# Two layer boundaries and the order of one VectorE step in a talking-heads attention with two MLPs

## The chip, the core and the metric

The kernel runs on one core of one Trainium2 chip. TensorE multiplies into PSUM, ScalarE and VectorE move and transform, GpSimd does a little elementwise work, and SyncE's queue issues nearly all DMAs. Each engine takes its instructions strictly in program order. The metric is device microseconds of one execution, median of 3 runs. A profiled execution adds a trace; its span leaves out the small time around the program.

## What is computed

```python
scores = scale * np.matmul(q, k.transpose(0, 1, 3, 2))     # 4 batches, 12 heads, 448 rows, 64 wide
scores = np.einsum('bhij,hg->bgij', scores, w_pre)         # heads mixed before the softmax
scores = scores - np.max(scores, axis=-1, keepdims=True)
attn = np.exp(scores)
attn = attn / (np.sum(attn, axis=-1, keepdims=True) + 1e-09)
attn = np.einsum('bhij,hg->bgij', attn, w_post)            # heads mixed after it
x = np.matmul(attn, v)                                     # -> 1792 rows of 768
h = x @ w_in;  g = np.where(h > 0, h, np.exp(np.minimum(h, 0)) - 1);  x = g @ w_out
h = x @ w_in2; r = np.maximum(h, 0); out = (r * r) @ w_out2       # both 768 -> 2048 -> 768
```

The MLP weights arrive as 64-bit floats, 768 x 2048 and 2048 x 768 for each of the two MLPs.

## The kernel before

**Attention** runs in T = 90 steps s of two row groups each. A step multiplies the pre-mix of step s+2 on TensorE (`mix_pre`, line 182, into two `ps_mix` banks; there are only two), then part of A·V of an earlier chunk (`values`, line 254), the post-mix of step s (`mix_post`, line 218, into two `ps_post` banks) and the scores of a later chunk (line 156). On VectorE a step holds, in program order: `weigh(s+1)`, which adds 1e-9 to the sums (`tot`, line 197) and takes their reciprocal (`rec`, line 199), after which GpSimd multiplies the mixing weights (`wg`, line 202); `maxima(s+2)`, two row maxima from `ps_mix` (`nmax`, line 190), after which ScalarE takes two exponentials (`ex`, line 192), which free the `ps_mix` banks for the next `mix_pre`; and the copies of the post-mix out of PSUM (`at`, line 236). At the end of a chunk ScalarE and VectorE also add up two A·V banks (`xs`, lines 262 and 263).

**The weights** are a list of units (`Weights`). A unit goes through `load` (DMA of the 64-bit words, `wd`), `size` (ScalarE, line 453), `turn` (four VectorE operations, lines 477 to 483, that make a 32-bit float `wf` of the 64-bit one), `part_hi` and `part_lo` (a high part `wh` cast by ScalarE, line 524, and the rest `wl` by VectorE, line 531). Each product is three matmuls: high x high, low x high, high x low (lines 670 to 672). `next()` calls `advance(i)` before unit i is used: it loads up to unit i+6, sizes up to i+5, turns up to i+4 and parts up to i+3, so the work of later units stands in the queues ahead of whatever the program does next. Turned units are also stored (`w1if<-wf`) for the second half of the rows.

**The first boundary.** In the last steps of the attention `plan` loads, sizes and turns units of the first MLP and multiplies the first two of them (`begin`, which takes both `ps_qk` banks). `inner(0)` then begins with output block f = 1 and unit 2; f = 0 is only activated (Relu and Exp on ScalarE, lines 690 and 692, then line 697 on VectorE, which frees the `ps_qk` bank that f = 2 takes next).

**The second boundary.** `outer_first` multiplies the hidden layer of the first half of the rows by w_out: six output blocks o, eight units each. After a block its two PSUM banks are split into the second MLP's input, `xh` (ScalarE, line 675) and `xl` (VectorE, line 676). `inner(1)` multiplies by the second MLP's units, k = 0 to 5 for each f, so its first f needs the split of o = 5 for k = 5. Beside both layers run 16 units of the last matrix (`load_beside`, `size_beside`): each is turned in step with another unit, which doubles the four operations of that `turn`.

Of the kernel before, what the change touches and what calls it, by code (L numbers as in the profile page):

```python
# [52 lines left out]
def attention(tc, dram, psum, qr, kr, vr, w_pre, w_post, diagonal, xd, mlps):  # L53
# [7 lines left out]
    with ExitStack() as ctx:  # L61
# [123 lines left out]
        def maxima(s):  # L185
            tot[s] = work.tile([128, 2], F32, name="tot", bufs=3)
            ex[s] = []
            for r, p in enumerate(mixed.pop(s)):
                nmax = work.tile([128, 1], F32, name="nmax", bufs=4)
                nc.vector.tensor_reduce(nmax, p, AX.X, ALU.max, negate=True)  # L190
                e = work.tile([128, S], F32, name="ex", bufs=2 * (MIX + 1))
                nc.scalar.activation(e, p, AF.Exp, bias=nmax, scale=1.0, accum_out=tot[s][:, r : r + 1])  # L192
                ex[s].append(e)

        def weigh(s):
            sums = tot.pop(s)
            nc.vector.tensor_scalar_add(sums, sums, 1e-9)
            rec = work.tile([128, 2], F32, name="rec", bufs=3)
            nc.vector.reciprocal(rec, sums)
            w = work.tile([128, 2, HALF], F32, name="wg", bufs=3)  # L200
            shape = [128, 2, HALF]
            nc.gpsimd.tensor_tensor(
                w, post.rearrange("p g r -> p (g r)").unsqueeze(1).broadcast_to(shape), rec.unsqueeze(2).broadcast_to(shape),
                ALU.mult,
            )
            wg[s] = w
# [60 lines left out]
        def store_x(s):  # L267
            while stored and stored[0][0] <= s:
                _, o, x = stored.pop(0)
                nc.sync.dma_start(out=o, in_=x)  # L270
# [74 lines left out]
        for s in range(T + 3):  # L345
            beside = extra.pop(s, ())
            pairs = [a for f, a in beside if f is scores]
            if s + 1 < T:
                weigh(s + 1)
            for x in gathers.get(s, ()):  # L350
                gather(x)
            if s + MIX < T:
                mix_pre(s + MIX)
                maxima(s + MIX)
            store_x(s)
            pieces = [a for f, a in beside if f is values]
            for a in pieces[:-1]:
                values(*a)
            if s < T:
                mix_post(s, 0)  # L360
            for a in pairs[:1]:
                scores(*a)
                keep_scores()
            if s < T:
                mix_post(s, 1)
                keep_weighed(s == T - 1)
            for a in pieces[-1:]:
                values(*a)
            for a in pairs[1:]:
                scores(*a, *((("pv", "pv"),) if s < values_from else ()))  # L370
                keep_scores()
            keep_x(s)
            for f, a in beside:
                if f not in (scores, values):
                    f(*a)
# [197 lines left out]
class Mlps:  # L573
# [25 lines left out]
    def plan(self, put, T, last, work, early_ctx, score_ctx):  # L599
        w = self.weights  # L600

        def start():
            early_ctx.close()
            score_ctx[2].close()
            score_ctx[1].close()
            self.xp = self.pool("xp", "right")
            self.tp = self.pool("tp", "right")
            self.nx = self.two_parts(KC, self.xp, "x", MOVING)
            self.xraw = {}

        def start_weights():
            score_ctx[0].close()
            w.pool = self.pool("wp", "right")
            w.pool.tile([128, 8], F32, name="room")
            self.raw_ctx = self.ctx.enter_context(ExitStack())
            w.raw_pool = self.pool("wr", "right", self.raw_ctx)

        for i in range(2):
            put(last - 8 + i, w.load, lambda: work.tile([128, 384, 2], I32, name="wd0", bufs=2))
            put(last - 5 + i, w.size, lambda: work.tile([128, 384], F32, name="wf0", bufs=2))  # L620
            for k in range(4):
                put(last - 4 + 2 * i + k // 2, w.turn_op, k)
        put(last, start)
        for i in range(2 * KC):
            put(last + i // 2, self.load_x, i)
            put(last + 3 + i // 2, self.split_x, i)
        put(last + 1, w.flush)
        put(T - 4, start_weights)
        for i in range(2):
            put(T - 4, w.part_hi)  # L630
            put(T - 4, w.part_lo)
            put(T - 3 + i, w.load)
            put(T - 1 + i, w.size)
            put(T - 1 + i, w.turn)
        for i in range(4):
            put(T - 3 + min(i, 2), self.begin, i)

# [213 lines left out]
    def outer_first(self, xh, xl, hh, hl):  # L851
        nc = self.nc
        for o in range(KC):
            p = [self.bank()[:, :S] for _ in self.BLOCKS]
            for f2 in range(FC // 2):
                wh, wl = self.weights.next()
                if f2 == 1:
                    self.weights.load_beside()
                if f2 == 4:
                    self.weights.size_beside()  # L860
                for j, bl in enumerate(self.BLOCKS):
                    for i in range(2):
                        f = 2 * f2 + i
                        self.three(p[j], wh[:, col(i)], wl[:, col(i)], hh[:, f, bl], hl[:, f, bl], f == 0, f == FC - 1)
            for j, bl in enumerate(self.BLOCKS):
                self.split(xh[:, o, bl], xl[:, o, bl], p[j])
# [233 lines left out]
    def run(self):  # L1100
        with ExitStack() as ctx:
            hp = self.pool("hp", "left", ctx)
            hh, hl = self.two_parts(FC, hp, "h", MOVING)
            self.inner(0, *self.nx, self.keep_parts(hh, hl))
            x = self.two_parts(KC, self.xp, "x", MOVING)
            self.outer_first(*x, hh, hl)
        self.hq = self.pool("hq", "left")
        w = self.weights

        def beside(f):  # L1110
            if f > 1 and w.aside:
                w.size_beside()
            if f % 3 != 2 and w.beside:
                w.load_beside(lambda: self.hq.tile([128, S + 32, 2], I32, name="wb", tag="rh", bufs=4))

        self.hr = {}
        self.start_split(STATIONARY)
        self.inner(1, *x, self.keep_raw, beside)
        x = self.outer_last(0)
        self.hr = {}  # L1120
        self.start_split(MOVING)
        self.seven(0, x)
        x, carry = self.outer_combos()
        self.hr = {}
        self.halves = {}
        self.seven(1, x, carry)
        self.seven_last()
# [49 lines left out]
```

## Time and profile before

| | us |
|---|---|
| median of 3 runs (lowest, highest) | 1265.84 (1263.19, 1271.76) |
| the profiled execution | 1264.1 |
| its span | 1262.3 |
| busy in the span: TensorE, VectorE, ScalarE, GpSimd | 1220.5, 990.5, 695.6, 52.5 |

A row of the timeline gives start, duration, engine and line, operation, output<-inputs, and in brackets how long the engine was idle before it and what it had waited for. Rows of one kind that follow each other are merged (x2). Matmuls overlap, so their durations are longer than the distance of their starts. TensorE's clock has two levels here, 2.4 GHz (granted clock 1.00) and 1.2 GHz (0.50); a stretch between shows both.

### The profile page before, as it was taken

The numbers are of one execution on the slowest core, as the hardware profiler recorded it, in microseconds if no ns is written. First come the engines' busy times: TensorE is split into PE (matmuls) and PEld (weight loads), VectorE is DVE, ScalarE is ACT, GpSimd is POOL, SyncE is SP. The second block draws the span as 40 slices with busy tenths as digits, with TensorE's granted clock in tenths as the row PEclk, the third lists the DMA queues.
The fourth block names the chain that finished last, engine by engine and source line by source line (L and its number), as shares of the span: only waits on it lengthen the run. The fifth ranks groups of instructions, "written<-read, shape, count | busy, mean of one in ns | idle before, by whom it ended". The sixth has DMA issues, their size and how long they took to land.

```text
span 1262.3 us, 35367 instructions
## 1 busy us (share of the span) xinstructions
PE 1220.5 (97%) x14223; PEld 1088.2 (86%) x14224; DVE 990.5 (78%) x2104; ACT 695.6 (55%) x1537; POOL 52.5 (4%) x118
## 2 busy tenths in 40 slices
PE   8899989999889999999899999999999999999998
PEld 4677667677679999998799999999999998999998
DVE  4576767677859998788899996868896758888876
ACT  4666666666637774333444454646673535455654
POOL 1010111011410000000000000000000000000000
PEclk9899999999999999999999999999999999999999
DMA  6665645655735545666666555222137441223443
GB/s 177 210 202 184 212 158 184 213 174 191 213 114 177 175 155 157 190 187 194 218 240 206 202 175 178 73 94 76 50 113 243 152 144 34 68 63 101 126 132 119
DMA packets 137948, 197.93 MB, mean 157 GB/s; under 512 B 26712, under 2 KB 117176, under 8 KB 137784
## 3 DMA queue, kind: packets, MB, share of 16 engines
q1 hardware_dynamic: 137544, 195.38, 48.4%
q8 instruction: 112, 1.84, 0.6%
q14 instruction: 52, 0.43, 0.1%
q10 hardware_dynamic: 240, 0.29, 0.1%
HBM read 114.44 MB, written 42.47 MB: 124 GB/s over the span
## 4 chain that ended last, share of the span: by engine, by line
PE 78%; DVE 11%; ACT 6%; issue 3%; DMA 1%; SPq 0%; ACTq 0%; DVEq 0%
PE ps_qk L670 5%; PE ps_qk L671 5%; PE ps_qk L672 5%; PE ps_pv L672 5%; PE ps_pv L671 5%; PE ps_post L670 5%; PE ps_mix L672 5%; PE ps_pv L670 5%; PE ps_mix L671 5%; PE ps_post L672 5%; PE ps_post L671 5%; PE ps_mix L670 5%; PE ps_mix L182 4%; PE ps_post L218 4%; PE ps_pv L254 4%; PE ps_qk L156 3%
## 5 line engine op out<-in xcount | busy, mean ns | idle before, releaser
L524 ACT CAST wh<-wf 128x384 fp32r<-128x384 f32 (+1 forms) x304 | 149.6, 494 | 196.9 <-DVE wf L483 129.0
L531 DVE TENSOR_TENSOR wl<-wf,wh 128x384 fp32r<-128x384 f32 (+1 forms) x304 | 162.4, 537 | 53.5 <-ACT wh L524 51.8
L218 PEld LDWEIGHTS ps_post<-wg,ex 60*64 60x64 f32 x5040 | 138.3, 135 | 51.8 <-issue 31.5
L192 ACT ACTIVATE ex<-ps_mix,nmax 128x448 f32<-128x448 f32 x180 | 112.6, 630 | 112.9 <-DVE nmax L190 112.7
L236 DVE COPY at<-ps_post 128x420 f32<-128x420 f32 x178 | 97.6, 591 | 56.8 <-PE ps_post L218 56.6
L218 PE MATMUL ps_post<-wg,ex 60*64 60x60 f32 x5040 | 134.2, 220 | 6.1 <-issue 3.8
L182 PE MATMUL ps_mix<-graw,pre 64*64 64x448 f32 (+1 forms) x720 | 111.6, 553 | 11.4 <-ACT ex L192 7.8
L190 DVE TENSOR_REDUCE nmax<-ps_mix 128x1 f32<-128x448 f32 x180 | 104.6, 617 | 19.8 <-PE ps_mix L182 19.4
L676 DVE TENSOR_TENSOR rl<-hr,rh 128x896 fp32r<-128x896 f32 (+2 forms) x104 | 94.8, 914 | 25.6 <-ACT rh L675 25.6
L675 ACT CAST rh<-hr 128x896 fp32r<-128x896 f32 (+2 forms) x104 | 82.9, 799 | 48.6 <-PE ps_post L672 24.7
L254 PE MATMUL ps_pv<-at,v 64*64 64x110 f32 (+3 forms) x2976 | 97.8, 248 | 4.2 <-issue 2.1
L254 PEld LDWEIGHTS ps_pv<-at,v 64*64 64x64 f32 x2976 | 86.6, 133 | 14.5 <-issue 5.8
L156 PE MATMUL ps_qk<-kt,qt 64*64 64x448 f32 (+1 forms) x680 | 92.4, 546 | 4.4 <-issue 3.2
L453 ACT ACTIVATE wf<-wd 128x384 f32<-128x384 f32 (+1 forms) x134 | 68.1, 513 | 42.3 <-DMA wd<-w1o 22.0
L161 ACT COPY sc<-ps_qk 120x448 f32<-120x448 f32 x167 | 80.7, 539 | 12.9 <-PE ps_qk L156 12.7
L483 DVE SCALAR_TENSOR_TENSOR wf<-wd,wf 128x384 int32<-128x384 int32 (+1 forms) x134 | 67.8, 510 | 3.9
L481 DVE SCALAR_TENSOR_TENSOR wf<-wd,wf 128x384 int32<-128x384 int32 (+1 forms) x134 | 67.8, 510 | 3.8
L690 ACT ACTIVATE tmp<-tmp 128x448 f32<-128x448 f32 x48 | 27.9, 580 | 58.1 <-DVE tmp L800 43.6
L182 PEld LDWEIGHTS ps_mix<-graw,pre 64*64 64x64 f32 (+1 forms) x720 | 34.8, 134 | 28.4 <-ACT ex L192 17.5
L670 PE MATMUL ps_qk<-xh,wh 128*128 128x448 f32 x150 | 55.3, 369 | 0.0
L671 PE MATMUL ps_qk<-xl,wh 128*128 128x448 f32 x150 | 55.0, 367 | 0.0
L672 PE MATMUL ps_qk<-xh,wl 128*128 128x448 f32 x150 | 54.9, 366 | 0.0
(286 smaller groups left out, 3179.6 us busy)
## 6 DMA issues: line engine op xcount, KB each, us to landing
graw<-sc SPq DMA_DIRECT2D x180, 210.0 KB
wd<-w1i SPq DMA_DIRECT2D x32, 384.0 KB
wd<-w1o SPq DMA_DIRECT2D x48, 256.0 KB
wd<-w2i SPq DMA_DIRECT2D x32, 384.0 KB
wf<-w2of SPq DMA_DIRECT2D x48, 192.0 KB
wd<-w2o SPq DMA_DIRECT2D x22, 384.0 KB
w1if<-wf SPq DMA_DIRECT2D x32, 192.0 KB
w1of<-wf SPq DMA_DIRECT2D x48, 128.0 KB
```

The costliest lines, as they stand in the source:

```text
L156: nc.tensor.matmul(out[a][x:y], qt[n][o, p, x:y], k[o, p, :], start=True, stop=True)
L182: nc.tensor.matmul(out[r][64 * g : 64 * g + 64], pre64[o], e[g][o], start=True, stop=True)
L190: nc.vector.tensor_reduce(nmax, p, AX.X, ALU.max, negate=True)
L192: nc.scalar.activation(e, p, AF.Exp, bias=nmax, scale=1.0, accum_out=tot[s][:, r : r + 1])
L218: nc.tensor.matmul(out[g][y, 6 if c == 3 else 2 * c + r], e[rows][o, key : key + 64], w[o, rows], start=True, stop=True)
L236: nc.vector.tensor_copy(o, p)
L254: nc.tensor.matmul(p, vt[b, i // 3][y, jc, g % 6 * D : (g % 6 + 1) * D], m, start=(jc == 0), stop=(jc == JC - 1), skip_group_check=True)
L524: self.nc.scalar.copy(hi, f)
L531: self.nc.vector.tensor_tensor(lo, self.single.pop(i), hi.bitcast(F32), ALU.subtract)
L670: mm(p, wh, xh, start=first, stop=False)
L671: mm(p, wh, xl, start=False, stop=False)
L672: mm(p, wl, xh, start=False, stop=last)
```

## The change

There are three edits. In the attention's loop `weigh(s+1)` moves behind `gather`, `mix_pre` and `maxima`. In `plan` three units instead of two are loaded, sized and turned in the attention's last steps, each one step earlier or at the same step, and two of them are also parted in step T - 1. In `outer_first` the last block's last unit is taken without `advance`, so that block's split stands ahead of the next layer's weights; the last block has no unit beside it, and `inner(1)` loads one unit more beside itself, in a changed rhythm.

```diff
         for s in range(T + 3):
...
-            if s + 1 < T:
-                weigh(s + 1)
             for x in gathers.get(s, ()):
                 gather(x)
             if s + MIX < T:
                 mix_pre(s + MIX)
                 maxima(s + MIX)
+            if s + 1 < T:
+                weigh(s + 1)
...
         for i in range(2):
             put(T - 4, w.part_hi)
             put(T - 4, w.part_lo)
-            put(T - 3 + i, w.load)
-            put(T - 1 + i, w.size)
-            put(T - 1 + i, w.turn)
+        for i in range(3):
+            put(T - 4 + i // 2, w.load)
+            put(T - 2 + i // 2, w.size)
+            put(T - 2 + i // 2, w.turn)
+        for i in range(2):
+            put(T - 1, w.part_hi)
+            put(T - 1, w.part_lo)
...
             for f2 in range(FC // 2):
-                wh, wl = self.weights.next()
-                if f2 == 1:
+                last = o == KC - 1 and f2 == FC // 2 - 1
+                if last:
+                    self.weights.load_ahead(self.weights.used)
+                    wh, wl = self.weights.take()
+                else:
+                    wh, wl = self.weights.next()
+                if f2 == 1 and o < KC - 1:
                     self.weights.load_beside()
-                if f2 == 4:
+                if f2 == 4 and o < KC - 1:
                     self.weights.size_beside()
...
-            if f % 3 != 2 and w.beside:
+            if f % 4 != 3 and w.beside:
                 w.load_beside(lambda: self.hq.tile([128, S + 32, 2], I32, name="wb", tag="rh", bufs=4))
```

TensorE's and GpSimd's rows stand in the same order in both kernels. The changed kernel's line numbers are higher by 4 from `begin` on and by 9 from `outer_first` on.

VectorE in one late attention step, before, from the sum of a chunk's end to the copies of the post-mix:

```order
L263 TENSOR_TENSOR xs<-xs,ps_pv 128x3x110
L197 TENSOR_SCALAR tot<-tot 128x2
L199 RECIPROCAL rec<-tot 128x2
L190 TENSOR_REDUCE nmax<-ps_mix 128x1 x2
L236 COPY at<-ps_post 128x84x5 x2
```

The same step in the changed kernel:

```order
L263 TENSOR_TENSOR xs<-xs,ps_pv 128x3x110
L190 TENSOR_REDUCE nmax<-ps_mix 128x1 x2
L197 TENSOR_SCALAR tot<-tot 128x2
L199 RECIPROCAL rec<-tot 128x2
L236 COPY at<-ps_post 128x84x5 x2
```

The addition and the reciprocal have moved behind the two maxima; the copies stay last.

ScalarE from the last split of the attention's end to the activation of f = 0, before (L453 sizes a unit, L524 casts a high part, L262 and L234 are the attention's last copies):

```order
L664 CAST xh<-tmp 128x448 x2
L234 COPY at<-ps_post 128x24x5 x2
L262 COPY xs<-ps_pv 128x3x110
L453 ACTIVATE wf<-wd 128x384
L262 COPY xs<-ps_pv 128x3x108
L262 COPY xs<-ps_post 128x3x108
L453 ACTIVATE wf<-wd 128x384
L524 CAST wh<-wf 128x384 x2
L453 ACTIVATE wf<-wd 128x384 x2
L524 CAST wh<-wf 128x384
L453 ACTIVATE wf<-wd 128x384
L690 ACTIVATE tmp<-ps_qk 128x448
```

The same stretch in the changed kernel:

```order
L668 CAST xh<-tmp 128x448 x2
L453 ACTIVATE wf<-wd 128x384 x2
L234 COPY at<-ps_post 128x24x5 x2
L262 COPY xs<-ps_pv 128x3x110
L453 ACTIVATE wf<-wd 128x384
L524 CAST wh<-wf 128x384 x2
L262 COPY xs<-ps_pv 128x3x108
L262 COPY xs<-ps_post 128x3x108
L453 ACTIVATE wf<-wd 128x384
L524 CAST wh<-wf 128x384
L453 ACTIVATE wf<-wd 128x384
L694 ACTIVATE tmp<-ps_qk 128x448
```

Units 2, 3 and 4 are sized, and units 2 and 3 cast, ahead of the attention's last two sums; behind them only units 5 and 6 are sized and unit 4 is cast before the activation.

VectorE at the end of `outer_first`, before, from the low part of unit 81 to that of unit 83 (L676 splits the last block):

```order
L531 TENSOR_TENSOR wl<-wf,wh 128x384
L477 TENSOR_SCALAR wf<-wf 128x384
L479 TENSOR_SCALAR wf<-wf 128x384
L481 SCALAR_TENSOR_TENSOR wf<-wd,wf 128x384
L483 SCALAR_TENSOR_TENSOR wf<-wd,wf 128x384
L531 TENSOR_TENSOR wl<-wf,wh 128x384
L477 TENSOR_SCALAR wf<-wf 128x384
L479 TENSOR_SCALAR wf<-wf 128x384
L481 SCALAR_TENSOR_TENSOR wf<-wd,wf 128x384
L483 SCALAR_TENSOR_TENSOR wf<-wd,wf 128x384
L676 TENSOR_TENSOR xl<-ps_mix,xh 128x448
L676 TENSOR_TENSOR xl<-ps_post,xh 128x448
```

The same place in the changed kernel, again from the low part of unit 81:

```order
L531 TENSOR_TENSOR wl<-wf,wh 128x384
L477 TENSOR_SCALAR wf<-wf 128x384
L479 TENSOR_SCALAR wf<-wf 128x384
L481 SCALAR_TENSOR_TENSOR wf<-wd,wf 128x384
L483 SCALAR_TENSOR_TENSOR wf<-wd,wf 128x384
L680 TENSOR_TENSOR xl<-ps_mix,xh 128x448
L680 TENSOR_TENSOR xl<-ps_post,xh 128x448
L531 TENSOR_TENSOR wl<-wf,wh 128x384
```

The split has moved ahead of the low part of unit 82 and the turn of unit 83. Those two, and on ScalarE the cast of unit 82 and the sizing of unit 84, now follow it.

## Rows read from the trace of the kernel before

**Rows 1.** Windows: PE, PEld, DVE, ACT, POOL busy (instructions), granted clock, DMA share, GB/s

```profile
20.00:348.00 328.00, 303.40 (x9171) 230.47 (x9168) 235.35 (x568) 214.47 (x577) 44.35 (x98) 0.99 0.61 195
...
592.00:660.00 68.00, 63.93 (x307) 58.18 (x306) 60.84 (x137) 31.19 (x66) 0.00 (x0) 0.97 0.66 226
```

**Rows 2.** Waits of PE, 20 to 347 us: total, times, longest

```profile
PE ps_mix L182 <- ACT ex L192: 7.8, 15, 0.9
```

**Rows 3.** Critical chain, 20 to 347 us, shares by line

```profile
by line: PE ps_mix L182 16.6%; PE ps_post L218 15.9%; PE ps_pv L254 12.5%; PE ps_qk L156 12.5%; ACT ex L192 9.6%; issue 6.4%; DVE nmax L190 5.3%; ACT sc L161 4.5%; DVE at L236 4.3%; DVE xs L263 2.8%; ACT xs L262 2.1%; DVE rec L199 1.4%; DMA
```

**Rows 4.** Critical chain, 168 to 170 us, in order of time: start, us

```profile
168.59 0.09 DVE tot L197
...
168.77 0.17 DVE rec L199
168.93 0.56 DVE nmax L190
```

**Rows 5.** Timeline of POOL at 321 us

```profile
321.58 0.39 POOL L202 TENSOR_TENSOR wg<-post,rec 128x120 f32<-128x120 f32 x1 [4.75 <-DVE rec L199]
```

**Rows 6.** Timeline of PE, 323 to 371 us

```profile
323.63 0.39 PE L218 MATMUL ps_post<-wg,ex 60*64 60x60 f32 x6
...
351.48 1.39 PE L218 MATMUL ps_post<-wg,ex 60*64 60x60 f32 x53 [1.39 <-DVE at L236]
...
366.66 0.47 PE L670 MATMUL ps_mix<-xh,wh 128*128 128x448 f32 x1 [1.36 <-ACT wh L524]
...
368.71 0.47 PE L672 MATMUL ps_mix<-xh,wl 128*128 128x448 f32 x1 [1.38 <-DVE wl L531]
...
370.18 0.58 PE L672 MATMUL ps_mix<-xh,wl 128*128 128x448 f32 x1
370.55 0.58 PE L670 MATMUL ps_post<-xh,wh 128*128 128x448 f32 x1
```

**Rows 7.** Timeline of DVE, 342 to 358 us

```profile
342.70 0.66 DVE L197 TENSOR_SCALAR tot<-tot 128x2 f32<-128x2 f32 x1
...
343.54 1.14 DVE L190 TENSOR_REDUCE nmax<-ps_mix 128x1 f32<-128x448 f32 x2
...
356.63 0.85 DVE L233 COPY at<-ps_post 128x300 f32<-128x300 f32 x2 [2.55 <-PE ps_post L218]
```

**Rows 8.** Timeline of ACT, 371 to 376 us

```profile
371.88 0.55 ACT L453 ACTIVATE wf<-wd 128x384 f32<-128x384 f32 x1 [3.15 <-DMA wd<-w1i]
373.87 0.56 ACT L453 ACTIVATE wf<-wd 128x384 f32<-128x384 f32 x1 [1.44 <-DMA wd<-w1i]
...
375.31 0.53 ACT L690 ACTIVATE tmp<-ps_qk 128x448 f32<-128x448 f32 x1
375.87 0.58 ACT L692 ACTIVATE tmp<-tmp 128x448 f32<-128x448 f32 x1
```

**Rows 9.** Timeline of PE, 600 to 605 us

```profile
600.05 0.36 PE L671 MATMUL ps_pv<-xl,wh 128*128 128x448 f32 x1
600.25 0.36 PE L672 MATMUL ps_pv<-xh,wl 128*128 128x448 f32 x1
603.38 0.47 PE L670 MATMUL ps_pv<-xh,wh 128*128 128x448 f32 x1 [2.77 <-ACT xh L675]
604.97 0.47 PE L671 MATMUL ps_pv<-xl,wh 128*128 128x448 f32 x1 [1.12 <-DVE xl L676]
```

**Rows 10.** Timeline of DVE, 595 to 605 us

```profile
595.73 0.62 DVE L477 TENSOR_SCALAR wf<-wf 128x384 f32<-128x384 f32 x2
...
597.74 1.02 DVE L483 SCALAR_TENSOR_TENSOR wf<-wd,wf 128x384 int32<-128x384 int32 x2
...
601.97 0.56 DVE L531 TENSOR_TENSOR wl<-wf,wh 128x384 fp32r<-128x384 f32 x1 [0.63 <-ACT wh L524]
602.44 0.35 DVE L477 TENSOR_SCALAR wf<-wf 128x384 f32<-128x384 f32 x1
...
604.30 0.62 DVE L676 TENSOR_TENSOR xl<-ps_mix,xh 128x448 fp32r<-128x448 f32 x1
```

## The prediction, made before the changed kernel ran

> **What bounds the kernel now.** I read the windows first, because the change touches three stretches. In the reader's order: from 20 to 348 us (attention) TensorE is busy 303.40 of 328.00 us, so it idles 24.6 us; from 592 to 660 us it idles 4.07 of 68 us and the granted clock is 0.97 instead of 1.00 [rows 1]. So an edit can only give back TensorE's idle time and, at the two boundaries, time spent at the lower clock.
>
> The waits say which idle time ended last on what the change moves. In the attention 15 waits of the pre-mix for the exponentials sum to 7.8 us, at most 0.9 each [rows 2]. An exponential waits for its row maximum, and the maximum stands on VectorE behind the addition and the reciprocal. The chain shows it: the addition begins at 168.59 and the maximum at 168.93, so the pair costs the chain 0.34 us a pass [rows 4]. The reciprocal has 1.4% of the chain's 327 us, 4.6 us at 0.17 each, hence 27 passes [rows 3].
>
> At the first boundary TensorE waits 1.36 us for unit 2's high part and 1.38 us for its low part, and then ten matmuls start 0.37 us apart (370.18, 370.55) [rows 6] where 0.20 is normal (600.05, 600.25) [rows 9]. At the second it waits 2.77 us for the last block's `xh` and 1.12 us for `xl` [rows 9], and then eight matmuls start 0.37 apart.
>
> **Edit 1, the reciprocal behind the maxima.** Nothing is added or removed; 90 additions and 90 reciprocals change place. Each of the 15 waits [rows 2] has at least one pass in the stretch ahead of it, so 15 x 0.34 = 5.1 us come off. Several stretches, those with a chunk's end in them, have two passes; two off every wait would clear nearly all 7.8 us. The upper bound is 27 x 0.34 = 9.2 us, if nothing else ends those stretches; the lower bound is about 2 us, if a ScalarE copy or a gather stands right behind. I take 5.1.
>
> Late in the attention GpSimd's splits run beside, and there one addition takes 0.66 us: from its start at 342.70 to the maximum at 343.54 are 0.84 us [rows 7]. That stretch ends in TensorE's wait of 1.39 us for the `at` copies at 351.48 [rows 6]. Moving the addition takes 0.8 off it.
>
> What this makes late is the reciprocal, by two maxima (1.14 us, the same length as at 343.54 [rows 7]), and with it `wg` on GpSimd. Queued behind it are only the `at` copies, whose total wait is unchanged, and on GpSimd the splits, which are ready earlier than they are needed. In one of the tightest steps `wg` ends at 321.58 + 0.39 = 321.97 [rows 5] and the post-mix that reads it starts at 323.63 [rows 6], so 1.66 us cover 1.14. Cost: nothing, with 0.5 us to spare.
>
> **Edit 2, three units ready in the attention.** Sizes and turns of units 2 and 3 move to step T - 2, where VectorE waits 2.55 us for TensorE before the copies at 356.63 [rows 7]. Two turns take 2 x 1.86 = 3.7 us (one turn lasts from 602.44 to 604.30 [rows 10]), so these copies and the chunk sum behind them come up to 1.2 us later. Their reader is the last `values`, which TensorE reaches only behind the 18 matmuls of `begin` (18 x 0.20 = 3.6 us), so the delay is covered. Unit 4's turn and the parts of 2 and 3 then fit into VectorE's next pause. So both waits at 366.66 and 368.71 go: TensorE would begin unit 2 at 366.66 - 1.36 = 365.30.
>
> What is late next is unit 4, needed 36 matmuls later: 365.30 + 36 x 0.20 = 372.5. Its cast stands behind the sizing of unit 5, and that load stands on SyncE's queue where unit 4's stood: behind the last stores of the attention, plus one more weight store. So I let unit 5 land when unit 4 did, at 371.88 [rows 8]; 0.55 for its sizing and 0.5 for the cast give 373.0. TensorE waits 0.5 us, and 0.2 more for the low part. After 9 more matmuls (1.8 us, at 375.0) it wants the `ps_qk` bank that the activation of f = 0 frees. The activation stands behind the sizing of unit 6, whose load I put at 373.87, where unit 5's was: 373.87 + 0.56 + Relu 0.53 + Exp 0.58 [rows 8] + 0.62 for a VectorE step of that size (as `xl` [rows 10]) = 376.2 and some hand-over, 376.3. TensorE waits 1.3 us. So of 1.36 + 1.38 + 10 x 0.17 = 4.4 us come back 4.4 - 2.0 = 2.4. Bounds: 4.4 if the loads land early, about zero if they land later and the clock falls as well.
>
> On the clock, what the rows show is that 2.7 us of idling in two pieces (with two matmuls between) was followed by the lower level, and the single 1.39 us at 351.48 was not [rows 6]. The two waits left here sum to 2.0 us with 1.8 us of matmuls between, so I count no fall. [...]
>
> **Edit 3, the split ahead of the next weights.** On VectorE the last block's `xl` loses what stood ahead of it: unit 82's low part and unit 83's turn, from 601.97 to 604.30, 2.33 us; and, since the last block has no unit beside it, the doubling of one turn, 3.03 us (595.73 to 597.74 + 1.02) against 1.86, so 1.2 us [rows 10]. It would begin at 604.30 - 2.33 - 1.2 = 600.8 and end at 601.4. TensorE wants `xh` at 600.61 (603.38 - 2.77 [rows 9]); ScalarE's casts, now ahead of unit 82's cast and unit 84's sizing, are ready for that. `xl` is wanted 0.2 later, so 0.6 to 0.7 us of wait remain. Of 2.77 + 1.12 + 8 x 0.17 = 5.25 us come back 4.6. Bounds: 5.3, and 3.2 if the clock falls even so.
>
> What is postponed returns in the next layer: the part of 82 and the turns of 83 and 84 follow at once. The two `xl` end at 601.9; by 1.86 per turn and 0.5 per low part unit 83 is ready at 601.9 + 0.5 + 2 x 1.86 + 0.5 = 606.6. TensorE reaches its low part 32 matmuls after it wanted `xh`: 600.61 + 0.7 + 32 x 0.20 = 607.7. Covered by 1.1 us; if VectorE comes later than that, TensorE waits for the excess. The extra unit in `inner(1)` is 1.2 us on VectorE, busy 60.84 of 68 there [rows 1]: hidden. The fewer loads in the last block only help.
>
> **Sum.** 5.1 + 0.8 + 2.4 + 4.6 = 12.9 us. The profiled execution of 1264.1 us (span 1262.3, and 1.8 around it) becomes 1251.2. It lies 1.7 us below the median of the runs, so I put the median at 1265.8 - 12.9 = 1252.9.
>
> **Rivals.**
> - *The first boundary only hands its wait on, with the clock.* For it: both remaining waits hang on loads that are issued no earlier than before. Against it: they are split by 1.8 us of work. The term falls to 0.7: 1254.6.
> - *The pair was not what held the attention.* For it: TensorE is busy 92% there, so a ScalarE copy or the matmuls themselves may follow close behind the maxima. Against it: the chain passes there 27 times. The term 5.9 falls to about 2: 1256.8.
> - *Two passes count at most waits.* The term 5.1 grows to 8 or 9: 1249.5.
> - *The postponed units are late.* Unit 83 misses its matmul by 1 us or more and the clock falls as well (1.4): the second boundary gives 2.2 instead of 4.6: 1255.3.
> - *Slower: `wg` becomes the wait.* Place: the post-mix of every step. Its cover in the tight steps is 1.66 - 1.14 = 0.5 us [rows 5, 6]. Each of 90 steps that then waits 0.15 us costs 13.5 us, so it decides once `wg` comes about 0.65 us later than I reckon in nearly all steps. With 0.3 us a step the time is 1265.8 - 12.9 + 27 = 1280. Against it: most steps have more cover than these.
>
> **How the numbers follow.** Chances: the forecast 0.45, two passes 0.13, the first boundary 0.15, the attention 0.15, postponed units 0.08, slower 0.04. About 1% (12.7 us) is what a measurement of this kernel can tell from no change, and the forecast lies on that edge: a little over half of its 0.45 is beyond it, with the two-pass case. That gives 0.43 faster by over 1%, 0.53 within, 0.04 slower. The range goes from 1247.5 (first terms near their upper bounds, 18 us) to 1260 (the lower bounds together, some 6 us), leaving out the slower case and the extremes.
>
> **What would show it.** In the trace after: `ps_mix` waits for `ex` at 3 us or less; no wait before unit 2; at unit 4 and at the `ps_qk` bank waits of 0.7 and 1.3 us at full clock; at the second boundary one wait under 1 us for `xl` and no fall of the clock; `wg` early in every step. The forecast is wrong if the pre-mix still waits 5 us or more, if the post-mix waits for `wg`, or if the matmuls behind either boundary start 0.37 us apart.

## The result and the profile after

| us | before | after |
|---|---|---|
| median of 20 runs each (lowest, highest) | 1269.15 (1262.72, 1277.93) | 1257.73 (1251.62, 1271.11) |
| the profiled execution, and its span | 1264.1, 1262.3 | 1261.62, 1259.8 |
| busy in the span: TensorE, VectorE, ScalarE, GpSimd | 1220.5, 990.5, 695.6, 52.5 | 1226.4, 989.7, 695.7, 52.7 |

The ratio of after to before is 0.991, with an interval of 0.9883 to 0.9938, a little under the 1% that the forecast put on its edge. The highest run of after counts as a slow one and is left out of the ratio. The medians lie 11.4 us apart, the two profiled executions only 2.5. TensorE even shows more busy time after, for the same matmuls. The section on the experiments explains that contradiction.

The windows of after answer to [rows 1]. The first is the attention up to the first matmul of `begin`, the others are the two boundaries (columns as there):

```profile
20.00:345.00 325.00, 302.49 (x9164) 228.75 (x9166) 235.28 (x568) 214.40 (x577) 44.76 (x98) 0.99 0.61 197
340.00:390.00 50.00, 47.32 (x717) 41.74 (x712) 35.68 (x78) 24.80 (x57) 6.46 (x8) 1.00 0.43 142
585.00:655.00 70.00, 69.77 (x338) 62.82 (x338) 63.12 (x147) 30.87 (x64) 0.00 (x0) 1.00 0.68 228
```

In the attention TensorE idles 22.5 us where it idled 24.6. At the second boundary it idles 0.23 us where it idled 4.07, and the granted clock is 1.00 at both.

TensorE's waits from 20 to 347 us after (total, times, longest) answer to [rows 2]:

```profile
PE ps_post L218 <- issue: 5.4, 10, 1.3
PE ps_pv L254 <- issue: 4.6, 6, 1.4
...
PE ps_mix L182 <- ACT ex L192: 2.2, 5, 0.8
PE ps_mix L182 <- issue: 1.9, 3, 0.8
...
PE ps_qk L156 <- issue: 0.5, 2, 0.3
```

and the rows for "issue" (a wait for nothing that the profile shows) before, which the prediction did not use:

```profile
PE ps_post L218 <- issue: 3.8, 7, 1.0
...
PE ps_qk L156 <- issue: 3.2, 3, 1.5
PE ps_pv L254 <- issue: 2.1, 3, 1.0
...
PE ps_mix L182 <- issue: 0.4, 1, 0.4
```

The wait for the exponentials fell from 7.8 to 2.2 us, in 5 places instead of 15. But "issue" rose from 9.5 to 12.4.

TensorE's timeline after, around the first boundary, answers to [rows 6] (+4 on the line numbers of the MLP):

```profile
348.14 1.39 PE L218 MATMUL ps_post<-wg,ex 60*64 60x60 f32 x53 [0.86 <-POOL wg L202]
...
362.79 0.47 PE L674 MATMUL ps_mix<-xh,wh 128*128 128x448 f32 x1
...
369.91 0.36 PE L676 MATMUL ps_post<-xh,wl 128*128 128x448 f32 x1
370.33 0.47 PE L674 MATMUL ps_pv<-xh,wh 128*128 128x448 f32 x1
370.64 0.37 PE L675 MATMUL ps_pv<-xl,wh 128*128 128x448 f32 x1
370.92 0.47 PE L676 MATMUL ps_pv<-xh,wl 128*128 128x448 f32 x1
371.23 0.37 PE L674 MATMUL ps_pv<-xh,wh 128*128 128x448 f32 x1
...
372.24 0.36 PE L676 MATMUL ps_pv<-xh,wl 128*128 128x448 f32 x1
373.31 0.47 PE L674 MATMUL ps_qk<-xh,wh 128*128 128x448 f32 x1 [0.72 <-DVE tmp L701]
373.62 0.36 PE L675 MATMUL ps_qk<-xl,wh 128*128 128x448 f32 x1
```

Unit 2 begins at 362.79 with no wait for its parts. Unit 4 begins at 370.33, and the four starts from 369.91 to 371.23 take 1.32 us where 0.80 is normal. The `ps_qk` bank is waited for 0.72 us. A new wait stands at 348.14, for `wg`, where the wait for `at` stood.

The same engine at the second boundary answers to [rows 9], and VectorE there to [rows 10]:

```profile
599.71 0.36 PE L674 MATMUL ps_pv<-xh,wh 128*128 128x448 f32 x1
600.30 0.47 PE L675 MATMUL ps_pv<-xl,wh 128*128 128x448 f32 x1 [0.23 <-DVE xl L680]
600.61 0.36 PE L676 MATMUL ps_pv<-xh,wl 128*128 128x448 f32 x1
600.81 0.36 PE L674 MATMUL ps_qk<-xh,wh 128*128 128x448 f32 x1
```

```profile
599.63 0.62 DVE L680 TENSOR_TENSOR xl<-ps_mix,xh 128x448 fp32r<-128x448 f32 x1
600.16 0.61 DVE L680 TENSOR_TENSOR xl<-ps_post,xh 128x448 fp32r<-128x448 f32 x1
600.69 0.55 DVE L531 TENSOR_TENSOR wl<-wf,wh 128x384 fp32r<-128x384 f32 x1
```

Of 2.77 and 1.12 us of waiting 0.23 is left. The split's low half stands ahead of the unit's low part, as the diff put it.

Starts of a few matmuls, from the traces, divide the time. "Before again" and "after again" are second profiles of the two kernels (below).

| us | before | before again | after | after again |
|---|---|---|---|---|
| first matmul of `begin` | 348.02 | 352.31 | 345.20 | 349.86 |
| from there to the first of f = 3 | 36.40 | 35.51 | 33.79 | 33.39 |
| first of block o = 5 to first of f = 1 in `inner(1)` | 34.32 | 34.74 | 27.76 | 28.55 |

### The profile page after: what moved, and what is told of

It is laid out like the page before. It is cut to its first block, busy times and chain, and to the rows that moved or that the text cites. A ratio compares the mean times of both kernels' runs of the same rounds, so it can differ in the third digit from the quotient of the medians.

```text
span 1259.8 us, 35368 instructions
## 1 busy us (share of the span) xinstructions
PE 1226.4 (97%) x14223; PEld 1083.8 (86%) x14224; DVE 989.7 (79%) x2104; ACT 695.7 (55%) x1537; POOL 52.7 (4%) x118
## 4 chain that ended last, share of the span: by engine, by line
PE 86%; DVE 5%; ACT 4%; issue 2%; DMA 2%; SPq 0%; POOL 0%; ACTq 0%; DVEq 0%; POOLq 0%
PE ps_qk L674 6%; PE ps_qk L676 6%; PE ps_qk L675 6%; PE ps_pv L675 6%; PE ps_pv L676 6%; PE ps_pv L674 6%; PE ps_mix L675 5%; PE ps_mix L676 5%; PE ps_post L674 5%; PE ps_mix L674 5%; PE ps_post L676 5%; PE ps_post L675 5%; PE ps_mix L182 5%; PE ps_post L218 5%; PE ps_pv L254 5%; PE ps_qk L156 4%
## 5 line engine op out<-in xcount | busy, mean ns | idle before, releaser
L524 ACT CAST wh<-wf 128x384 fp32r<-128x384 f32 (+1 forms) x304 | 149.5, 494 | 196.5 <-DVE wf L483 128.7
L453 ACT ACTIVATE wf<-wd 128x384 f32<-128x384 f32 (+1 forms) x133 | 67.5, 512 | 49.0 <-DMA wd<-w1o 22.1
L156 PE MATMUL ps_qk<-kt,qt 64*56 64x448 f32 (+1 forms) x680 | 91.9, 545 | 1.7 <-ACT sc L161 1.1
L182 PEld LDWEIGHTS ps_mix<-graw,pre 64*64 64x64 f32 (+1 forms) x720 | 34.3, 134 | 25.0 <-ACT ex L192 10.3
L676 PE MATMUL ps_qk<-xh,wl 128*128 128x448 f32 x150 | 54.8, 365 | 0.0
```

What stands on the lines that cost most here:

```text
L156: nc.tensor.matmul(out[a][x:y], qt[n][o, p, x:y], k[o, p, :], start=True, stop=True)
L182: nc.tensor.matmul(out[r][64 * g : 64 * g + 64], pre64[o], e[g][o], start=True, stop=True)
L524: self.nc.scalar.copy(hi, f)
L676: mm(p, wl, xh, start=False, stop=last)
```

## The experiments

Two theories are called C and D in the texts on record. They concern the distance between the starts of 448-column matmuls, which after the restart at 373.31 is 0.2067 us in the first profile of after, and stays so until 714.27: 1,647 matmuls x 0.0067 = 11.0 us. In the first profile of before it is 0.2000 in all these stages. By C the change (its wait for the `ps_qk` bank) brings the longer distance; by D it comes and goes with the execution, in either kernel.

**One edit at a time.** Three kernels hold one edit each, made as in the diff ahead of the prediction, and nothing else:

```diff
-            if s + 1 < T:
-                weigh(s + 1)
             for x in gathers.get(s, ()):
...
                 maxima(s + MIX)
+            if s + 1 < T:
+                weigh(s + 1)
```

> Only edit 1: the reciprocal behind the maxima; the rest is as before. Theory A (the order takes the 0.34 us pair off the chain): the pre-mix's waits for the exponentials fall from 7.8 us to about 2, the first MLP matmul starts at 344 to 346 us instead of 348.02, and the time falls by 3 to 5 us; both boundaries show the waits of before (2.7 us and 3.9 us, and the low clock behind each). Rival B (nothing real comes of the order; the 2.8 us between the two traces there are the chance of TensorE's own issue waits): start within 1 us of 348.02, time the same. Open beside these: whether matmuls of 448 columns start 0.200 or 0.207 us apart behind the boundaries; 1700 matmuls at 0.207 cost 11 us and would hide either.

Measured: ratio 0.9972 (0.9946 to 0.9998), 1267.27 us beside 1270.26. The pre-mix waits 4.0 us for the exponentials, TensorE 15.4 for "issue", and `begin` starts at 345.75. At the end of the attention it waits 1.4 us for `wg`, so that new wait belongs to edit 1. The start and the 3 to 5 us of theory A came; the low clock that the text expected behind both boundaries came behind the second alone.

```diff
-            put(T - 3 + i, w.load)
-            put(T - 1 + i, w.size)
-            put(T - 1 + i, w.turn)
+        for i in range(3):
+            put(T - 4 + i // 2, w.load)
+            put(T - 2 + i // 2, w.size)
+            put(T - 2 + i // 2, w.turn)
+        for i in range(2):
+            put(T - 1, w.part_hi)
+            put(T - 1, w.part_lo)
```

> Only edit 2: three units made ready in the attention. Theory A: the two waits before unit 2 (1.36 and 1.38 us) and the low clock go, one wait for the ps_qk bank of 0.5 to 1.5 us comes; from the first MLP matmul to the first one of output block 3 it takes 33 to 34 us instead of 36.4, time 2 to 3 us less. Rival B (the wait is only handed on, with the clock): 35.5 us or more for that stretch, time the same within 1 us. Attention and second boundary as before.

Measured: ratio 0.998 (0.9954 to 1.0006), 1266.34 us. From `begin` to f = 3 are 33.05 us, 3.4 less than before's 36.40 and 2.5 less than before again's 35.51; the bank wait of 0.7 us is there, and the second boundary waits as before (3.0 for `xh`, 0.8 for `xl`).

```diff
-                wh, wl = self.weights.next()
-                if f2 == 1:
+                last = o == KC - 1 and f2 == FC // 2 - 1
+                if last:
+                    self.weights.load_ahead(self.weights.used)
+                    wh, wl = self.weights.take()
+                else:
+                    wh, wl = self.weights.next()
+                if f2 == 1 and o < KC - 1:
                     self.weights.load_beside()
...
-            if f % 3 != 2 and w.beside:
+            if f % 4 != 3 and w.beside:
```

> Only edit 3: the last block's split ahead of the next weights, no unit beside that block. Theory A (the larger part of the gain is here): from the first matmul of the last block of the first MLP to the first of output block 1 of the second it takes about 27 us instead of 34.3; waits there under 0.5 us, no low clock; time 6 to 8 us less. Rival B (worth what was predicted, 4.6 us): 29.5 us or more. Attention and first boundary as before.

Measured: ratio 0.9976 (0.9951 to 1.0001), 1266.46 us. From o = 5 to f = 1 are 27.76 us, and the only wait there is the following one (waits of TensorE, 570 to 660 us).

```profile
PE ps_pv L671 <- DVE xl L676: 0.3, 1, 0.3
```

The stretch is near theory A's 27 us, but its 6 to 8 us did not come in the time of a run: 0.9976 is 3.0 us, and the interval reaches to 6.2.

So each wait goes with the edit that was meant for it, and no edit needs another. The low clock behind the second boundary goes with edit 3 too: it stands in the traces of all four executions without that edit (before, before again, edit 1 alone, edit 2 alone) and in none of the eight with it. The three ratios add up to 0.72% off, all three together measure 0.9%; with half-intervals of 0.25 each, that is the same. The distance between matmuls speaks against C here: the kernel with edit 3 alone has before's first boundary and yet 0.2067 in `inner(0)` and `outer_first`; those with edit 1 or 2 alone have it in `inner(1)`, behind before's stalls.

**Both kernels profiled once more.**

> The kernel before, unchanged, profiled once more, for the distance between 448-column matmul starts at full clock (0.2000 us in every MLP stage of the first profile of it). Theory D (the distance is drawn anew at a restart of TensorE, in each execution, whatever the kernel): some stage of inner(0), outer_first or inner(1) may show 0.2067 us here too, and the span differs from the first profile's 1262.3 by about 3.9 us for each such stage, besides the attention's own scatter of 2 or 3 us. Theory C (the changed kernel's wait at the ps_qk bank sets it): 0.2000 in all stages again. The attention's TensorE waits for instructions sum to 9 to 13 us again.

> The changed kernel, unchanged, profiled once more. Theory D: its stages show another pattern than 0.2067 in all three of inner(0), outer_first and inner(1); with none at 0.2067 the span is 1259.8 - 11.5 = 1248.3 or so, with one of the three about 1252. Theory C: 0.2067 in all three again, from the wait of about 0.7 us for the ps_qk bank on, and a span of 1259 to 1261. In both the waits of the pre-mix for the exponentials sum to 3 us or less, those for instructions to 11 to 13, and the post-mix waits about 0.9 us for wg at the end of the attention.

Measured: the kernel before has 0.2000 in `inner(0)` and 0.2067 throughout `inner(1)` this time; TensorE's timeline there:

```profile
615.17 0.37 PE L670 MATMUL ps_mix<-xh,wh 128*128 128x448 f32 x1
615.38 0.37 PE L671 MATMUL ps_mix<-xl,wh 128*128 128x448 f32 x1
615.59 0.37 PE L672 MATMUL ps_mix<-xh,wl 128*128 128x448 f32 x1
```

The kernel after, in `inner(0)`, in its first profile:

```profile
400.07 0.37 PE L674 MATMUL ps_post<-xh,wh 128*128 128x448 f32 x1
400.28 0.37 PE L675 MATMUL ps_post<-xl,wh 128*128 128x448 f32 x1
```

and in its second, behind the same bank wait (0.71 us):

```profile
377.74 0.47 PE L674 MATMUL ps_qk<-xh,wh 128*128 128x448 f32 x1 [0.71 <-DVE tmp L701]
...
400.05 0.36 PE L674 MATMUL ps_post<-xh,wh 128*128 128x448 f32 x1
400.25 0.36 PE L675 MATMUL ps_post<-xl,wh 128*128 128x448 f32 x1
```

C falls: the same wait is followed by either distance, and the kernel before shows the longer one too. Over the 12 profiled executions of this case, 9 of 36 stages (`inner(0)`, `outer_first`, `inner(1)`) run at 0.2067 from end to end, three of them in the first profile of after. That is why it hid the gain, though not by all of the 11.0 us. From the first matmul of f = 3 to 714.27 it takes 335.3 us, after again 327.6: 7.7 us more. At 0.2000 `outer_first` has small waits for its units (1.6 us in after again, a quarter of it besides at the longer distance), and at 0.2067 none. 1261.62 less 7.7 is 1253.9. After again takes 1258.42 and not the 1250 that D gave: its attention is 4.7 us longer, more than the 2 or 3 us of scatter that the text on record allowed, and the small waits are back. The longer attention shows in TensorE's waits of after again from 340 to 392 us:

```profile
PE ps_mix L182 <- issue: 3.2, 1, 3.2
PE ps_post L218 <- POOL wg L202: 1.4, 1, 1.4
```

The wait of 3.2 us ends at 343.32, the granted clock from 340 to 350 us is 0.83 there, where it is 1.00 in the first profile, and the "issue" waits from 20 to 347 us sum to 16.0, not to the 11 to 13 expected. Before again takes 1273.08: its `begin` starts 4.3 us later than in the first profile (a wait of 2.1 us for "issue" at 337.43, with a granted clock of 0.83 from 335 to 345 us), and its `inner(1)` is 3.8 us longer. Some 8 us for three long stages and 5 for the attention are most of the 15 us between the lowest and the highest run of before; that sum is argued, since single runs leave no trace.

Before again shows one thing more. Its first boundary waits 1.36 and 1.36 us for unit 2, as in the first profile, yet the next matmuls start 0.20 us apart (373.40, 373.61, 373.81), at a granted clock of 1.00 from 360 to 380 us. So do those of edit 1 alone, of edit 3 alone and of the split alone (below). The low clock of [rows 6] stands in one of the five executions with the old units.

**The two parts of edit 3.** The split alone, without the unit taken from beside the last block; of edit 3 these lines stay as before:

```diff
                 if f2 == 1:
                     self.weights.load_beside()
                 if f2 == 4:
                     self.weights.size_beside()
...
             if f % 3 != 2 and w.beside:
```

> Edit 3 without its unit beside: the split stands ahead of the next layer's weights, but the last block of outer_first still loads and turns a unit beside itself, so one turn is doubled there (3.03 us in place of 1.86). If both parts of the edit count as I reckoned, xl comes 1.2 us later than with the whole edit (which waited 0.3 us for it), TensorE waits 1.3 to 1.6 us for xl, and from the first matmul of the block o = 5 to the first of f = 1 it takes 29 us (34.3 before, 27.8 with the whole edit, with its part at 0.2067 us). If the order alone does it, the wait for xl stays at 0.5 us or less and the stretch at 27.8 or less. Span 1258 to 1266.

Measured: 29.31 us from o = 5 to f = 1, and in TensorE's waits from 570 to 660 us

```profile
PE ps_pv L671 <- DVE xl L676: 1.1, 1, 1.1
PE ps_pv L670 <- ACT wh L524: 0.6, 1, 0.6
```

Both parts count. The order alone takes 5.0 of the 34.3 us off; with the doubled turn that stays in the last block `xl` is waited for 1.1 us, where the seven executions with the whole edit wait 0.2 to 0.6. The wait of 0.6 for a high part has nothing to do with it: it stands at 571.09, ahead of the last block, and after again has one of 0.4 at the same matmul. The wait for `xl` predicted by adding both parts up (1.3 to 1.6) was a little too long.

**The late `wg`.** Why it is late at 348.14 stands in VectorE's rows after (and GpSimd's, which takes `rec` at 347.64):

```profile
343.95 2.13 DVE L531 TENSOR_TENSOR wl<-wf,wh 128x384 fp32r<-128x384 f32 x2 [0.84 <-ACT wh L524]
346.01 1.14 DVE L190 TENSOR_REDUCE nmax<-ps_mix 128x1 f32<-128x448 f32 x2
347.08 0.16 DVE L197 TENSOR_SCALAR tot<-tot 128x2 f32<-128x2 f32 x1
347.33 0.17 DVE L199 RECIPROCAL rec<-tot 128x2 f32<-128x2 f32 x1
```

Two low parts of 2.13 us stand ahead of the maxima, and unit 1's is not needed until `begin`'s third call, two steps on. A kernel puts it one step later:

```diff
         for i in range(2):
-            put(T - 4, w.part_hi)
-            put(T - 4, w.part_lo)
+            put(T - 4 + i, w.part_hi)
+            put(T - 4 + i, w.part_lo)
```

> The changed kernel, with unit 1 of the weights split into its high and low part one attention step later (its first matmul is two steps later). That takes one of the two low parts (1.1 us) on VectorE, and one of the two casts on ScalarE, from ahead of the last two row maxima. If these low parts are what makes the last wg late (the theory), the post-mix's wait of 0.86 us for wg goes, and begin's second matmul and all behind it come 0.8 us earlier: from begin's first to f = 1's first matmul 16.8 us in place of 17.6, and the median 0.5 to 1 us under the changed kernel's, a ratio of 0.9905, with the interval too wide to tell it from 0.991. If instead the pair of addition and reciprocal behind the maxima is what makes it late, the wait shrinks by no more than 0.3 us. If the addition before the next reciprocal now stands behind the low part, wg's next user waits 0.3 us or more instead, and nothing is gained.

Measured: ratio 0.9902 (0.9866 to 0.9939), 1253.82 us beside 1265.99. TensorE's waits from 340 to 392 us, all of them:

```profile
PE ps_mix L182 <- issue: 3.7, 1, 3.7
PE ps_qk L674 <- DVE tmp L701: 0.7, 1, 0.7
```

The wait for `wg` is gone from the list, and from `begin` to f = 1 are 16.39 us: 0.85 less than in after again (17.24), about as predicted, and 1.2 less than in after (17.59), which has an "issue" wait of 0.6 there besides. `wg` ends 2.07 us behind the first matmul of `begin`, where it ended 2.83 behind it in after. The theory holds; in the time of a run 0.001 of a ratio cannot be told.

**The bank wait.** f = 0's activation, which frees the bank, stands ahead of the sizing of units 5 and 6:

```diff
+            if begun:
+                weights.take(), weights.take()
+                for j, bl in enumerate(self.BLOCKS):
+                    keep(m, f, bl, p[j])
+                weights.advance(0)
+                weights.advance(1)
+                continue
```

> The changed kernel, but the activation of output block 0 stands ahead of the sizing of units 5 and 6 in the queues, so that the ps_qk bank is free in time. Theory A (the bank's wait of 0.72 us hangs on the sizing's loads): that wait goes and no other of over 0.5 us comes in its place; unit 4's cast, behind unit 5's load, is the next. Theory C (the wait is also what makes the following matmuls start 0.207 us apart instead of 0.200): without it 0.200 holds through the first MLP, which is worth up to 11 us against an execution with 0.207. Rival D (which of the two distances holds is a matter of chance in each execution, whatever wait came before): 0.207 can still show, and the median is within 2 us of the changed kernel's, some 11 us under before.

Measured: ratio 0.9911 (0.9876 to 0.9946), 1258.17 us beside 1270.26, as the changed kernel. In the trace the wait of 0.72 is gone; a wait of 0.3 us for a high part comes in its place, and from f = 1 to f = 3 are 15.24 us, 1.0 less than in after (16.20). From `begin` to f = 3 are 31.62 us (after 33.79), but the other 1.2 lie between `begin` and f = 1, which this kernel leaves as it was: in this execution TensorE stopped for 2.1 and 1.7 us of "issue" ahead of `begin`, and `wg` was in time.

**Both of these together.**

> The changed kernel with unit 1's parts one step later and, in addition, the activation of f = 0 ahead of the sizing of units 5 and 6. The two remaining waits of the first boundary, 0.86 us for wg and 0.72 us for the ps_qk bank, both go, at the price of some waits of 0.2 to 0.6 us for the parts of units 5 and 6: from begin's first matmul to that of f = 3 about 31 us (33.8 in the changed kernel, 32.3 with the parts moved alone). If those waits are real time, the ratio to before is 0.9895 to 0.9905; if the postponed sizing costs as much as it frees, it is 0.991 as for the changed kernel.

Measured: ratio 0.988 (0.9837 to 0.9922), 1256.13 us beside 1270.08. Neither wait is left, and from `begin` to f = 3 are 30.76 us, 3.0 less than in after. This is the lowest ratio of all, yet its interval overlaps that of the changed kernel: the shorter stretch is shown, that the whole is faster than the changed kernel is not.

**Edit 1 undone, the others kept.**

> The changed kernel with edit 1 undone: the addition and the reciprocal stand ahead of the maxima again, the units and the split stay. In the profiles so far TensorE's waits for the exponentials fell with edit 1 from 6.7 to 3.2 us (means of five executions each), but its waits for instructions rose from 11.1 to 14.3, and begin came 2.8 us earlier. If edit 1 is worth about 3 us also beside the other two, the ratio to before is 0.9935 (against 0.991 with it), the pre-mix waits 5 to 8 us for the exponentials and the waits for instructions in the attention sum to 9 to 13 us. If edit 1 is worth nothing (the waits for instructions take all of it), the ratio is 0.991. At the boundaries: one wait of about 0.7 us for the ps_qk bank and one of about 0.5 us for xl, no fall of the clock, but in the tail the wait for wg is replaced by one for the exponentials or the at copies.

Measured: ratio 0.9928 (0.9899 to 0.9957), 1261.72 us. TensorE's waits from 20 to 347 us:

```profile
PE ps_mix L182 <- ACT ex L192: 8.9, 16, 1.2
PE ps_post L218 <- issue: 5.9, 7, 1.8
...
PE ps_pv L254 <- issue: 2.8, 3, 1.2
...
PE ps_qk L156 <- issue: 1.1, 2, 0.7
...
PE ps_mix L182 <- issue: 0.3, 1, 0.3
```

The exponentials' waits are back (8.9), "issue" is down to 10.1, and at the end the `at` copies are waited for again, 1.4 us. Beside the other two, edit 1 is worth 0.9928 - 0.991 = 0.0018, 2.3 us; alone it was 0.0028, 3.6 us. Neither says much of its size: alone the interval stops just short of 1, at 0.9998, and the two intervals that 2.3 comes from overlap widely. The traces of all 12 executions say more (means, lowest to highest; the waits are those of TensorE from 20 to 347 us, and the 86th of the 90 pre-mixes is a mark inside the attention):

| us | six without edit 1 | six with it |
|---|---|---|
| pre-mix waiting for exponentials | 7.1 (5.1 to 8.9) | 3.1 (2.2 to 4.0) |
| all "issue" waits | 10.9 (9.5 to 13.2) | 14.1 (12.4 to 16.0) |
| of these, up to the 86th pre-mix | 9.1 (8.2 to 10.1) | 10.1 (7.5 to 12.0) |
| first matmul of the 86th pre-mix | 332.3 (330.6 to 333.9) | 327.9 (325.7 to 329.1) |
| from there to the first matmul of `begin` | 17.6 (15.9 to 22.0) | 20.0 (16.8 to 21.6) |
| first matmul of `begin` | 350.0 (347.4 to 355.0) | 347.9 (345.2 to 350.4) |

Up to the 86th pre-mix the waits do become time: TensorE is 4.4 us ahead there, all six executions with edit 1 are ahead of all six without it, and "issue" has grown by only 1.0. In the last steps 2.3 of the 4.4 are lost again on the mean. "Issue" grows from 2.2 to 4.3 us there, in single waits of up to 3.7 us, some with the low clock behind them, as in after again. Before again has such a wait too and the ranges overlap, so it is not shown that edit 1 brings them. What TensorE waits for in an "issue" wait no row names; that stays open.

## Point by point

**The sum.** Forecast 12.9 us, measured 11.4; the forecast of 1252.9 is 4.8 us under the measured median. Of that, 3.3 us are the median of the kernel before, 1269.15 in these runs where the three shown gave 1265.84, and 1.5 us are the sum. That the sum is so near is in part luck, since its errors have opposite signs: the attention gave some 2 to 3.6 us of the 5.9 forecast, the two boundaries some 8 of 7.0. Of the chances, 0.43 less the 0.13 for two passes leaves 0.30 of the 0.45, two thirds and not "a little over half".

**Edit 1.** 5.1 predicted; 4.4 gained up to the 86th pre-mix, 2.1 left at `begin`, 2.3 and 3.6 in the times of whole runs. The mechanism was right, and so was the step from the waits to the path, "15 x 0.34 = 5.1 us come off", nearly to its size, as far as that mark: 3 us or less of waits were said, and 2.2 and 3.3 came in the two profiles of after. What the sum had wrong is the end of the attention, where it counted on another 0.8 and 2.3 are lost on the mean, in "issue" waits; these are 6.4% of the chain in [rows 3], and the prediction read past them. The lower bound of "about 2 us, if a ScalarE copy or a gather stands right behind" is near what is left at `begin`, but for another reason.

**The late step of the attention.** "Cost: nothing, with 0.5 us to spare" for `wg` held in the inner steps (no such wait from 20 to 347 us in either profile of after), but not in the last one, which I had treated under the `at` copies alone. There the wait of 1.39 for `at` became one for `wg`, of 0.86 in after, 1.44 in after again and 1.42 with edit 1 alone. So 0.5 of the 0.8 came in the first of these and nothing in the others. A wait of the post-mix for `wg` was one of the prediction's signs that the forecast is wrong; it came, in one step of 90. Reading that one step, with the two low parts ahead of the maxima, would have shown it.

**Edit 2.** Predicted 2.4 for the first boundary. Over the executions with the old units (before, before again, and those with edit 1 or 3 or the split alone) `begin` to f = 3 takes 36.2 us, over the four with the new ones and otherwise like after (after twice, edit 2 alone, edit 1 undone) 33.4: 2.8. Without the split alone, which has a granted clock of 0.87 from 360 to 370 us, it is 35.8 and 2.4. The units' waits went, as said. The 10 x 0.17 = 1.7 us of low clock that the term counts as won back are in the first profile of before alone; the three others take 35.5 to 35.8 without it. (Unit 3 is loaded, sized and turned two steps earlier, not one as the section on the change has it.) Unit 4 was said to cost 0.7 and by the starts cost 0.5 (0.7 in after again); the wait for the bank was said to be 1.3 and was 0.7, for this reason, in ScalarE's rows after:

```profile
369.33 0.55 ACT L453 ACTIVATE wf<-wd 128x384 f32<-128x384 f32 x1 [6.01 <-DMA wd<-w1i]
369.78 0.49 ACT L524 CAST wh<-wf 128x384 fp32r<-128x384 f32 x1
370.60 0.55 ACT L453 ACTIVATE wf<-wd 128x384 f32<-128x384 f32 x1 [0.32 <-DMA wd<-w1i]
371.05 0.53 ACT L694 ACTIVATE tmp<-ps_qk 128x448 f32<-128x448 f32 x1
```

Unit 5's load, which I let land where unit 4's had, at 371.88 [rows 8], landed 2.55 us sooner, at 369.33; TensorE began unit 2 at 362.79, 2.5 earlier than my 365.30. The order of waits was right and each shifted with the start of the stretch, which I had held fixed for the loads: unit 5 lands 24.1 us behind the first matmul of `begin` in after and 23.9 behind it in after again, as unit 4 did in before (23.9).

**The clock.** No fall was predicted at the boundaries and none came: 1.00 in both windows, with waits of 0.86, some 0.2 and 0.72 us at the first boundary. But the row that the prediction argued from, 2.7 us of idling in two pieces with the lower level behind it, is one execution of five; behind the same two waits the clock stayed at 1.00 in the other four. What decides is open.

**Edit 3.** Predicted 4.6, measured 5.5 where the distances are nearly alike: 34.32 before, and 28.84 to 28.89 in the four further kernels with edits 2 and 3, which have most of this stretch at 0.2000 us. (After, with 27.76, has all of it at 0.2067, after again, with 28.55, most.) The wait left was put at 0.6 to 0.7 us for `xl`; it was 0.23 in the one profile and 0.5 in the other. What was too small is the price of a stop: the matmul behind 372.24 should start at 372.44, and with the named wait of 0.72 at 373.16; it starts at 373.31 and the next 0.31 later instead of 0.20, 0.26 us in all beyond the wait's own number. Of that, 0.16 is waiting which the bracket leaves out, since it counts from the end of the row ahead, 0.36 behind its start, where the next matmul would start 0.20 behind it; 0.11 is the longer distance after the stop. Before, there were two such stops, so the 5.25 us were some 0.5 too few. The postponed unit 83 was in time, as the margin of 1.1 us said: no wait for it in either profile of after. The cost of the extra unit in `inner(1)` did not show.

**The rivals.** "The pair was not what held the attention" comes nearest by its total, 1256.8, 0.9 from the measured median, but its reason is wrong: the pair did hold the attention, for 4.4 us up to the 86th pre-mix, and what made the term small came at the end. "Two passes" (8 or 9 us) is refuted by the same 4.4. "The first boundary only hands its wait on" put that boundary at 0.7 (2.4 less the 1.7 of low clock), where 2.4 to 2.8 came; "the postponed units are late" is refuted by the rows above. The slower rival's place was right in one step of 90, at 0.86 and 1.44 us.

## What to carry to other kernels

A wait that falls is not yet time: give the change a mark inside the loop, and compare several executions there and at the end. Here the gain stands clear of the scatter at the 86th of 90 steps, and half of it is gone on the mean at the end, where single waits of another kind stand. Where a step is moved for the mean of many repetitions, read the first and the last one by themselves, since there something else stands in the queue. Before two profiled executions are compared, compare the distance of like instructions in a stretch that the change does not touch; a difference there belongs to the execution. Before a low clock is counted as won back, look for it in a second execution of the same kernel.

## What the hardware showed that was not expected

At a granted clock of 1.00, matmuls of 448 columns start either 0.2000 or 0.2067 us apart, for whole stages of 500 matmuls and more. In the seven traces followed for this nearly every change from one to the other stands at a stop of 0.3 to 6 us. Both kernels show it. In the profile's pages it looks like a busier engine: from 395 to 465 us both kernels show 70.00 us busy of 70.00, in their first profiles with 351 matmuls before and 341 after. What picks the distance is open. Behind a stop the first distance is 0.31 us instead of 0.20.

The clock behind like waits was not alike either: two waits of 1.36 to 1.38 us with two matmuls between were followed by the lower level in one execution of five, while waits of 2.8 to 3.0 us with another of 0.6 to 1.1 behind them were followed by it in four of four.
